# A first transfer and a narrow transfer: w2 ahead of wq, and the tail of w1 on 16 partitions

## The chip, the cores and the metric

The kernel runs on one core of one Trainium2 chip. The metric is the device time of one execution in microseconds (us). The six runs of the kernel before lie between 214.81 and 215.13 us (0.15%). A transfer into on-chip memory goes to partitions (the 128 rows of a tile). In the traces it is carried in packets, and most transfers end on 16 DMA engines (the last one of w4 leaves 16 landing records, from 209.43 to 211.38 us).

## The reference, cut to what matters

A decode step for 4 sequences: attention over the last 2048 positions of a cached K and V, plus a small MLP branch. The outputs are summed.

```python
xn = layernorm(x)                                   # x: [4, 1, 576]
out = x + A(xn, k_cache, v_cache, wq, wo) + B(xn, w1, w2, w3, w4)
# A: q = xn @ wq (576 x 4096); 32 query heads, 16 KV heads of 128; softmax; @ wo
# B: h = gelu(layernorm(x) @ w1)                    # w1: 576 x 576
#    pads and slices of h along S = 1, then @ w2    # w2: 576 x 576
#    x1 = x + ...;  x1 + gelu(layernorm(x1) @ w3) @ w4
```

With S = 1 the shifted slices of h are zero, so the product with w2 uses a zero operand. The kernel still loads w1 and w2 and does the matmuls. About 88.5 MB are read, and nearly all of it is K and V.

## The kernel before: the parts that matter

Each engine has a list of operations, sorted by `key`. One queue (SP) issues almost all transfers, in the order of their keys. Weights with 576 rows are split into 512 rows, four per partition, and a tail of 64 rows. The tails of w1 and w2 share one tile: w1's rows on even partitions, w2's on odd ones.

```python
w1main = w4_t[:, 0:4 * D].rearrange("p (r n) -> p r n", r=4)      # D = 576
rag12 = w4_t[:, 8 * D:9 * D]
...
def rag_pair(tile, even, odd):
    return [(tile[p:128:2, 0:w.shape[1]], w[512:576, :]) for p, w in enumerate((even, odd))]
...
ev_wq = [add_dma([(kt_t[:], A_wq[0:512, :].rearrange("(p r) n -> p (r n)", r=4))], "wq", (), -60),
         add_dma(rag_pair(ragq3, B_w3, A_wq), "wqr", ["ragq3_zero"], -59)]
ev_r12 = add_dma(rag_pair(rag12, B_w1, B_w2), "r12", (), -58.5)
ev_w2 = add_dma([(w2main, B_w2[0:512, :].rearrange("(p r) n -> p r n", r=4))], "w2", (), -58)
ev_w3 = add_dma([...], "w3", (), -57)
ev_w1 = add_dma([...], "w1", (), -56)
... # then K (16 transfers of 2 MB), V (16), wo (2), w4 (5, of falling size)

def pe_h(h):                      # h = xn2 @ w1, half h of the columns
    def f(e):
        for r in range(4):
            e.matmul(HTps[h], lhsT=xn2T[:, r, :], rhs=w1main[:, r, HALF * h:HALF * (h + 1)], start=(r == 0), stop=False)
        return e.matmul(HTps[h], lhsT=xn2T[:, 4, :], rhs=rag12[:, HALF * h:HALF * (h + 1)], start=False, stop=True)
    return f
```

## Time and profile before

| | before |
|---|---|
| time, median of 6 runs | 214.96 us |
| span of the profiled run | 213.6 us |
| share of 16 DMA engines' span, queue 1 | 97.8% |
| bytes read | 88.49 MB |
| landings of the last w4 transfer on its 16 engines: first, mean, last | 209.43, 210.40, 211.38 us |

The page of the kernel before, in 40 slices of 5.3 us: the digits are busy tenths (9 is 90% or more); the GB/s row is what the DMA engines moved; then come the DMA queues with packets, MB and share.

```profile
DMA  7999989999999999999999999999999999999993
GB/s 270 418 380 507 442 359 436 417 428 423 426 430 426 423 430 436 422 430 426 433 426 430 430 422 427 430 420 433 430 423 426 430 433 426 426 429 439 422 406 130
...
q1 hardware_dynamic: 6520, 88.50, 97.8%
q8 instruction: 8, 0.13, 0.2%
q14 instruction: 2, 0.02, 0.0%
```

The DMA row is unbroken. What ends last is therefore a DMA engine, and the chain of waits says so (start, length, what):

```profile
178.09 32.22 DMA w<-in_B_w_dram
210.31 0.04 issue
210.36 1.40 PE ps L431 x18
211.75 0.43 DVE out_sb L548
```

The timeline of before shows the first issues, q's matmuls, the second pass with w3 (it waited 2.0 us for w3), the first K transposes, and at the end the weight load that waited for the last packet of w4:

```profile
0.81 0.41 SPq L176 DMA_DIRECT2D kt<-in_A_wq_dram  x1
13.42 3.60 PE L293 MATMUL ps<-kt,xnT 128*32 128x512 bf16 x32
28.51 4.70 PE L511 MATMUL ps<-w,x1nT 128*32 128x387 bf16 x69 [2.04 <-DMA w<-in_B_w_dram]
36.36 1.95 PE L333 MATMUL ps<-perm_bf,ring 128*128 128x128 bf16 x32
...
211.42 0.08 PEld L431 LDWEIGHTS ps<-w,h2T_sb 128*4 128x4 bf16 x2 [0.24 <-DMA w<-in_B_w_dram]
```

The averages of the page hide one thing. The trace also records every DMA packet (start, duration, size) and every landing (read here as one per DMA engine and transfer: 16 records for w2 or w3; five for x, four of them at 7.91 to 8.27 us and one at 3.16 us, before its data moved at 6.32). On one engine, each packet starts 3 or 4 ns before the one ahead of it ends, so a packet chain can be followed. In these traces each engine is then a serial worker with fixed periods: 47 ns for a packet of 1152 bytes, 174 ns for 4608, 0.61 us for 16 KB, about 1.22 us for 32 KB. A late engine doesn't catch up: the spread of the landings stays between 1.93 and 1.98 us from the K transfer at 49 us to the end. The 16 landings of the last w4 transfer, in ns after the first of them, were:

```
before: 0 18 28 199 257 367 377 856 1405 1520 1583 1620 1645 1833 1909 1951
```

The kernel ends with the slowest of these 16. The two large groups in that list come from the instruction queue (q8 in the page): each 16 KB packet of it sets one engine back by about 1.55 us.

### The profile page before, as it was taken

How to read it: one execution, taken by the hardware profiler on the slowest of the kernel's cores; microseconds unless marked ns; L12 is line 12 of the kernel's file. 1: busy time of each engine (PE TensorE's matmuls, PEld its weight loads, DVE VectorE, ACT ScalarE, POOL GpSimd, SP SyncE). 2: the span in 40 equal slices, each digit the busy share in tenths (PEclk: the TensorE clock that was granted, in tenths of full speed). 3: DMA queues.
4: the chain of work that ended last, by engine and by line, in shares of the span. 5: the costliest groups of instructions: out<-in, count | busy, mean ns of one | idle time of the engine just before them, and what ended most of it. 6: DMA issues, size and time to landing. Idle time of an engine off the chain costs nothing. (4 is left out here: it accounts for less than half of the span.)

```text
span 213.6 us, 5903 instructions
## 1 busy us (share of the span) xinstructions
PE 142.3 (67%) x2664; PEld 110.4 (52%) x2668; DVE 75.2 (35%) x147; ACT 61.8 (29%) x76; POOL 10.9 (5%) x38
## 2 busy tenths in 40 slices
PE   0058469999999999999996178033444433336995
PEld 0023256877778887888874058033434433334542
DVE  0332701666666666666664840100010001001000
ACT  2001204666555665666666530000000000000000
POOL 8301000000000000000000000000000000000000
PEclk9999959999999999999999555555555555555799
DMA  7999989999999999999999999999999999999993
GB/s 270 418 380 507 442 359 436 417 428 423 426 430 426 423 430 436 422 430 426 433 426 430 430 422 427 430 420 433 430 423 426 430 433 426 426 429 439 422 406 130
DMA packets 6546, 88.65 MB, mean 415 GB/s; under 512 B 764, under 2 KB 1032, under 8 KB 1544
## 3 DMA queue, kind: packets, MB, share of 16 engines
q1 hardware_dynamic: 6520, 88.50, 97.8%
q8 instruction: 8, 0.13, 0.2%
q14 instruction: 2, 0.02, 0.0%
q10 hardware_dynamic: 16, 0.01, 0.0%
HBM read 88.49 MB, written 0.00 MB: 414 GB/s over the span
## 5 line engine op out<-in xcount | busy, mean ns | idle before, releaser
L333 PE MATMUL ps<-perm_bf,ring 128*128 128x128 bf16 x1024 | 62.5, 219 | 1.3 <-PEq L572 0.3
L333 PEld LDWEIGHTS ps<-perm_bf,ring 128*128 128x128 bf16 x1024 | 57.5, 98 | 10.7 <-issue 10.7
L340 DVE COPY kt<-ps 128x1024 bf16<-128x1024 bf16 x80 | 52.3, 687 | 27.2 <-PE ps L333 27.2
L339 ACT ACTIVATE kt<-ps 128x1024 bf16<-128x1024 bf16 x48 | 49.2, 1024 | 30.8 <-PE ps L333 29.5
L414 PE MATMUL ps<-PTpad,ring 128*128 128x8 bf16 x1024 | 29.6, 168 | 41.2 <-PEq L572 37.6
L414 PEld LDWEIGHTS ps<-PTpad,ring 128*128 128x128 bf16 x1024 | 28.7, 104 | 42.3 <-issue 42.2
L549 ACT ACTIVATE out_sb<-ps 4x288 bf16<-4x288 f32 x1 | 0.4, 402 | 87.2 <-PE ps L431 87.2
L347 PE MATMUL ps<-kt,Qs 128*32 128x512 bf16 x272 | 17.8, 382 | 1.4 <-PEq L572 1.4
L403 DVE TENSOR_TENSOR PTpad<-PT,mU_bf 128x512 bf16<-128x512 bf16 x16 | 6.4, 421 | 29.4 <-PE ps L414 29.4
L426 DVE TENSOR_TENSOR OTn<-ps,rinvB 128x32 bf16<-128x32 f32 x4 | 0.8, 191 | 34.5 <-PE ps L414 34.5
L347 PEld LDWEIGHTS ps<-kt,Qs 128*32 128x32 bf16 x272 | 5.7, 95 | 6.8 <-issue 1.5
L274 PE MATMUL ps<-ident_bf,xn_bf 4*128 4x4 bf16 x8 | 0.6, 170 | 12.9 <-DVE ragsrc L268 12.9
L368 POOL COPY Qs<-Qpad 128x128 bf16<-128x128 bf16 x16 | 4.6, 296 | 86.9 <-PE ps L347 73.6
L511 PE MATMUL ps<-w,x1nT 128*32 128x387 bf16 (+7 forms) x90 | 5.9, 404 | 2.3 <-DMA w<-in_B_w_dram 2.0
L274 PEld LDWEIGHTS ps<-ident_bf,xn_bf 4*128 4x128 bf16 x8 | 0.4, 112 | 12.9 <-issue 10.5
L511 PEld LDWEIGHTS ps<-w,x1nT 128*32 128x32 bf16 x90 | 4.5, 124 | 3.6 <-DMA w<-in_B_w_dram 2.3
L431 PE MATMUL ps<-w,ORT 128*4 128x288 bf16 x64 | 5.5, 345 | 0.4 <-DVE ORT L453 0.4
L548 DVE CAST out_sb<-ps 4x288 bf16<-4x288 f32 x1 | 0.4, 446 | 14.5 <-PE ps L431 14.5
L431 PE MATMUL ps<-w,h2T_sb 128*4 128x288 bf16 x72 | 5.0, 286 | 0.7 <-DMA w<-in_B_w_dram 0.7
L385 PE MATMUL ps<-kt,permT_bf 128*128 128x512 bf16 x3 | 1.8, 607 | 4.9 <-DVE kt L384 4.8
L261 ACT ACTIVATE sd<-mv 4x1 f32<-4x1 f32 x3 | 0.6, 202 | 14.8 <-DVE mv L259 14.8
L431 PEld LDWEIGHTS ps<-w,ORT 128*4 128x4 bf16 x64 | 3.3, 102 | 2.9 <-DVE ORT L453 1.0
(99 smaller groups left out, 65.8 us busy)
## 6 DMA issues: line engine op xcount, KB each, us to landing
ring<-in_A_k_cache_dram SPq DMA_DIRECT2D x16, 2048.0 KB, 14.5
ring<-in_A_v_cache_dram SPq DMA_DIRECT2D x16, 2048.0 KB, 17.4
w<-in_B_w_dram SPq DMA_DIRECT2D x1, 4608.0 KB, 24.0
w<-in_A_wo_dram SPq DMA_DIRECT2D x2, 2304.0 KB, 20.9
kt<-in_A_wq_dram SPq DMA_DIRECT2D x1, 4096.0 KB, 12.3
w<-in_B_w_dram SPq DMA_DIRECT2D x1, 2592.0 KB, 28.0
w<-in_B_w_dram SPq DMA_DIRECT2D x3, 576.0 KB, 13.7
w<-in_B_w_dram SPq DMA_DIRECT2D x1, 1296.0 KB, 30.6
```

The source lines that it names most:

```text
L274: e.transpose(XTps[idx][:, r, :], v[:, r, :], ident_bf[0:B, 0:B])
L333: ins = e.transpose(tb[n % 4][:, t, :], slot_t(c)[:, 8 * k + t, :], perm_bf[:])
L339: return "act", lambda e: e.activation(out=ktbuf[:, n % 16], in_=tb[n % 4], func=ACTF.Copy)
L340: return "dve", lambda e: e.tensor_copy(out=ktbuf[:, n % 16], in_=tb[n % 4])
L347: ins = e.matmul(Sps[32 * u:32 * u + 32, q, :].rearrange("p (t i) -> p t i", t=16), lhsT=Qs[:, c % NPOS, 32 * u:32 * u + 32], rhs=ktgrp[:, ...
L368: P(lambda e, c=c, cc=cc: e.tensor_copy(out=Qs[:, c % NPOS, :], in_=Qpad_t[:, 128 * cc:128 * cc + 128]), waits=["qT", "qs_zero"] + ([f"SC{ ...
L385: add("pe", lambda e, q=q: e.matmul(ps[:, 4 + q % 3, :], lhsT=permT_bf[:], rhs=PTx[:, q, :], start=True, stop=True), waits=[f"PTx{q}", "pe ...
L403: return lambda e: e.tensor_tensor(out=PTpad[:, c % 2], in0=PTv[:, :, cc, :].unsqueeze(2).to_broadcast([128, NT, NU, 2]), in1=mU_bf[:].uns ...
L414: ins = e.matmul(o_, lhsT=slot_t(c)[:, t, :], rhs=PTpad[:, c % 2, t].rearrange("p u e -> p (u e)"), start=(t == 0), stop=(t == NT - 1))
L426: add("dve", lambda e, hv=hv: e.tensor_tensor(out=hv(OTn), in0=OTps.rearrange("p (b h) -> p b h", b=B), in1=hv(rinvB), op=ALU.mult), waits ...
L431: return e.matmul(ACC[h], lhsT=lhsT, rhs=rhs, start=start, stop=stop, tile_position=(0, 32 * h), skip_group_check=True)
L511: ins = e.matmul(H2ps[k][32 * g:32 * g + 32, :].rearrange("p (x c) -> p x c", c=9)[:, :, off:off + cnt], lhsT=x_, rhs=w[:, base_:base_ + 1 ...
```

## The change

Its intent is to have small packets first, and to take bytes off the DMA engines that end last. It has two parts. w2's 512 rows are issued first. The 64 last rows of w1 go to 16 partitions (4 rows on each), read with an outermost dimension of 4. The second part needs more matmuls of 16 rows each, more transposes, and a memset of the tile that w2's tail now has alone.

```diff
+        w1rag = w4_t[0:16, 18 * D:22 * D]
...
-        xn2T = sb("xn2T", [128, 5, B], BF16)
+        xn2T = sb("xn2T", [128, 8, B], BF16)
...
+        P(lambda e: e.memset(rag12[:], 0.0), sig="rag12_zero", key=-98)
...
-        ev_r12 = add_dma(rag_pair(rag12, B_w1, B_w2), "r12", (), -58.5)
-        ev_w2 = add_dma([(w2main, ...)], "w2", (), -58)
+        ev_r12 = add_dma([(w1rag, B_w1[512:576, :].rearrange("(b a c) n -> a b (c n)", b=4, a=4)),
+                          (rag12[1:128:2, :], B_w2[512:576, :])], "r12", ["rag12_zero"], -58.5)
+        ev_w2 = add_dma([(w2main, ...)], "w2", (), -61)
...   (the last 64 columns of xn2 are reordered to match; 4 transposes of 16 columns replace 1 of 128)
-                return e.matmul(HTps[h], lhsT=xn2T[:, 4, :], rhs=rag12[...], start=False, stop=True)
+                for c in range(4):
+                    ins = e.matmul(HTps[h], lhsT=xn2T[0:16, 4 + c, :], rhs=w1rag[:, c * D + HALF * h:c * D + HALF * (h + 1)],
+                                   start=False, stop=(c == 3))
```

More of the change, by code (lines that the diff above doesn't have):

```diff
@@ L146, in bass_parallel_sum__sliding_block_cached__mixer_s_mlp__decode_kernel @@
         HTps = [ps[0:B, 2 + k, 0:HALF] for k in range(2)]
-        XTps = [ps[:, k, a:a + 10].bitcast(BF16).rearrange("p (c b) -> p c b", b=B) for k, a in ((3, 300), (7, 0), (7, 12))]
+        XTps = [ps[:, k, a:a + 16].bitcast(BF16).rearrange("p (c b) -> p c b", b=B) for k, a in ((3, 300), (7, 0), (7, 20))]
         S = {}
@@ L218, in bass_parallel_sum__sliding_block_cached__mixer_s_mlp__decode_kernel @@
                  add_dma(rag_pair(ragq3, B_w3, A_wq), "wqr", ["ragq3_zero"], -59)]
-        ev_r12 = add_dma(rag_pair(rag12, B_w1, B_w2), "r12", (), -58.5)
-        ev_w2 = add_dma([(w2main, B_w2[0:512, :].rearrange("(p r) n -> p r n", r=4))], "w2", (), -58)
+        ev_r12 = add_dma([(w1rag, B_w1[512:576, :].rearrange("(b a c) n -> a b (c n)", b=4, a=4)),
+                          (rag12[1:128:2, :], B_w2[512:576, :])], "r12", ["rag12_zero"], -58.5)
+        ev_w2 = add_dma([(w2main, B_w2[0:512, :].rearrange("(p r) n -> p r n", r=4))], "w2", (), -61)
         ev_w3 = add_dma([(w3_t[:], B_w3[0:512, :].rearrange("(p r) n -> p (r n)", r=4))], "w3", (), -57)
@@ L266, in ln_ops @@
                                                  op0=ALU.subtract, op1=ALU.mult), waits=[f"{tag}_rstd"], sig=f"{tag}_n", key=k0 + 0.04)
-            odd = int(idx == 0)
-            add("dve", lambda e: e.tensor_copy(out=ragsrc[:, idx, odd:128:2], in_=dst[:, 512:D]), waits=[f"{tag}_n", "rag_zero"], sig=tag, key=k0 + 0.05)
+            r_out, r_in = ragsrc[:, idx, int(idx == 0):128:2], dst[:, 512:D]
+            if idx == 1:
+                r_out = ragsrc[:, idx, 0:64].rearrange("q (c a b) -> q c a b", c=4, a=4)
+                r_in = r_in.rearrange("q (b a c) -> q c a b", b=4, a=4)
+            add("dve", lambda e: e.tensor_copy(out=r_out, in_=r_in), waits=[f"{tag}_n", "rag_zero"], sig=tag, key=k0 + 0.05)
         def pe_xT(src, idx):
@@ L274, in f @@
                     e.transpose(XTps[idx][:, r, :], v[:, r, :], ident_bf[0:B, 0:B])
-                return e.transpose(XTps[idx][:, 4, :], ragsrc[:, idx, :], ident_bf[0:B, 0:B])
+                if idx != 1:
+                    return e.transpose(XTps[idx][:, 4, :], ragsrc[:, idx, :], ident_bf[0:B, 0:B])
+                for c in range(4):
+                    ins = e.transpose(XTps[idx][0:16, 4 + c, :], ragsrc[:, idx, 16 * c:16 * c + 16], ident_bf[0:B, 0:B])
+                return ins
             return f
@@ L280, in bass_parallel_sum__sliding_block_cached__mixer_s_mlp__decode_kernel @@
         add("pe", pe_xT(xn_bf, 0), waits=["ident_bf", "ln1"], sig="xT", key=-40)
-        add("dve", lambda e: e.tensor_copy(out=xnT[:, :, 0:B], in_=XTps[0]), waits=["xT", "xnT_zero"], sig="xnT", key=-39)
+        add("dve", lambda e: e.tensor_copy(out=xnT[:, :, 0:B], in_=XTps[0][:, 0:5, :]), waits=["xT", "xnT_zero"], sig="xnT", key=-39)
         def pe_q(r):
@@ L313, in bass_parallel_sum__sliding_block_cached__mixer_s_mlp__decode_kernel @@
         add("pe", pe_xT(xn2_bf, 1), waits=["ln2", "ident_bf"], sig="x2T", key=-36)
-        add("dve", lambda e: e.tensor_copy(out=xn2T[:], in_=XTps[1]), waits=["x2T"], sig="xn2T", key=-25)
+        add("dve", lambda e: e.tensor_copy(out=xn2T[:, 0:4, :], in_=XTps[1][:, 0:4, :]), waits=["x2T"], sig=None, key=-25)
+        add("dve", lambda e: e.tensor_copy(out=xn2T[0:16, 4:8, :], in_=XTps[1][0:16, 4:8, :]), waits=["x2T"], sig="xn2T", key=-24.9)
         def pe_zero(e):
@@ L471, in f @@
                     e.matmul(HTps[h], lhsT=xn2T[:, r, :], rhs=w1main[:, r, HALF * h:HALF * (h + 1)], start=(r == 0), stop=False)
-                return e.matmul(HTps[h], lhsT=xn2T[:, 4, :], rhs=rag12[:, HALF * h:HALF * (h + 1)], start=False, stop=True)
+                for c in range(4):
+                    ins = e.matmul(HTps[h], lhsT=xn2T[0:16, 4 + c, :], rhs=w1rag[:, c * D + HALF * h:c * D + HALF * (h + 1)], start=False, stop=(c == 3))
+                return ins
             return f
@@ L490, in bass_parallel_sum__sliding_block_cached__mixer_s_mlp__decode_kernel @@
         add("pe", pe_xT(x1n_bf, 2), waits=["ln3", "xn2T"], sig="x1T", key=-23)
-        add("dve", lambda e: e.tensor_copy(out=x1nT[:, :, 0:B], in_=XTps[2]), waits=["x1T", "x1nT_zero"], sig="x1nT", key=-23)
+        add("dve", lambda e: e.tensor_copy(out=x1nT[:, :, 0:B], in_=XTps[2][:, 0:5, :]), waits=["x1T", "x1nT_zero"], sig="x1nT", key=-23)
         for h in range(2):
```

## The prediction

> **What bounds the kernel.** The 16 DMA engines. The DMA row of the 40 slices is 9 in all but three slices, queue 1 takes 97.8% of 16 engines' span, and the windows view shows a DMA share of 0.96 to 1.01 until 178 us. The packet records show no engine idle between the first packets (1.8 to 2.3 us) and the last landings (209.4 to 211.4 us). The chain of waits ends in 32 us of w4 transfer, 1.4 us of last matmuls, 0.43 us of copy, then the output. The time is start, plus the packets of the slowest DMA engine, plus that tail.
>
> The engines do not end together: the 16 landings of the last w4 transfer spread over 1.95 us. A 16 KB packet of the instruction queue (8 in the trace) sets the one engine that carries it back by about 1.55 us, an 8 KB one by 0.6 to 1.0 us, and this is never made up.
>
> **What the change does, in DMA.** Bytes are equal. Order: w2 (8 packets of 4608 bytes per engine, 174 ns apart, 1.4 us) goes ahead of wq. The tail of w1 was 4 packets of 1152 bytes on each of 16 engines (47 ns apart, 0.19 us); now it is 16 packets of 4608 bytes. [...] No trace has shown this transfer yet; the load of x (4 packets of 1152 bytes) is one that uses 4 engines. So four engines get 4 x 174 = 0.70 us instead of 0.19 (+0.51 us), twelve get 0.19 us less. Following the packets end to start, the four engines of x end about 0.4, 0.9, 1.4 and 1.6 us after the first of the last landings, one less certain; the latest (1.95) is not among them. Estimate: the latest moves from 1.95 to about 2.1 (1.6 + 0.51), +0.1 to +0.2 us; -0.19 if none of the four is late, up to +0.5 if one is among the very latest.
>
> w2 first: the first packet of each engine takes 1.6 to 2.2 us for what later takes 1.22. I take that excess as a start latency any first packet pays: 0, give or take 0.15 us.
>
> **What it does on the engines.** q waits for wq: its matmuls start at 13.4 us, so q, its transposes, hs and ln3 come about 1.4 us later. The second h2 pass waits for w3 anyhow (28.5 us, 2 us idle before it), so this is hidden; w3 itself lands within 0.5 us of before. The tail of w1 takes 8 matmuls instead of 2 (about 0.2 us each at the reduced clock), 3 more transposes, one more copy (0.15 us): K transposes start 1 to 2 us after 36.3. Slot 0 then is free near 43 us instead of 41.2; the fourth K transfer lands at 49 us, so the queue never runs dry. The added memset on POOL (about 0.6 us) ends before SP reaches its wait. Nothing of this is on the critical path.
>
> **Prediction.** 215.0 us, 8 in 10 between 214.6 and 215.5. Faster by over 2%: 0.01; within 2%: 0.98; slower: 0.01.
>
> **What would show it.** Sixteen 4608-byte packets for the tail of w1, on four engines; w1's landings spread wider by 0.7 us (four late); the DMA row unbroken; q's matmuls near 14.8; h2's second pass near 28.5 to 29; the last w4 landing 0.1 to 0.2 us later.
>
> **What would make it wrong.** Instruction packets landing on other engines; a first transfer of small packets starting noticeably faster or slower; writes to 16 partitions being slower than 174 ns a packet.

The number of engines of the new tail was the author's assumption, with the load of x as the nearest thing in the trace of before (four packets, and the landings told above). 214.85 us (the median of the three runs known then), plus about 0.15 (1.6 + 0.51 against 1.95), plus 0 for the start, is 215.0.

## The result, and the profile after

| | time, median (runs) | before in the same rounds | ratio, 95% interval |
|---|---|---|---|
| after, first measured | 214.77 us (6) | 214.96 us (6) | 0.9990 (0.9977 to 1.0003) |
| after, measured again (e10) | 214.73 us (5) | 215.04 us (9) | 0.9985 (0.9972 to 0.9999) |

All ratios here are the mean time of one kernel's runs over that of the other's of the same rounds, so they are not quite the ratio of the medians quoted. The time fell by 0.2 to 0.3 us, one part in a thousand. That is close to the noise: the first interval includes no change, the second just excludes it. The time lies inside the predicted range. The predicted shift, however, was upward (214.85 was the median of the three runs known then, 215.0 predicted), and the measured one is downward: the range was wide enough to hold both. Two steps of the forecast were wrong, and the experiments were made to find them.

The page of after, the same rows:

```profile
DMA  7999999999999999999999999999999999999993
GB/s 295 406 398 477 435 382 439 418 428 421 436 424 424 430 436 421 422 436 427 427 427 439 421 438 419 427 421 427 433 430 427 424 430 427 436 431 419 434 408 117
...
q1 hardware_dynamic: 6460, 88.50, 97.7%
q8 instruction: 8, 0.13, 0.2%
q14 instruction: 2, 0.02, 0.0%
```

The bytes are the same, in 60 packets fewer. The first slice moves 295 GB/s instead of 270. The timeline of after:

```profile
0.81 0.41 SPq L177 DMA_DIRECT2D w<-in_B_w_dram  x1
2.24 0.58 POOL L197 MEMSET w<- 128x576 bf16 x1
14.46 3.17 PE L303 MATMUL ps<-kt,xnT 128*32 128x512 bf16 x32
28.51 4.88 PE L524 MATMUL ps<-w,x1nT 128*32 128x387 bf16 x69 [2.92 <-DMA w<-in_B_w_dram]
37.33 1.95 PE L344 MATMUL ps<-perm_bf,ring 128*128 128x128 bf16 x32
...
211.25 0.08 PEld L442 LDWEIGHTS ps<-w,h2T_sb 128*4 128x4 bf16 x2 [0.22 <-DMA w<-in_B_w_dram]
```

q starts 1.0 us later. The second w3 pass starts at the same 28.51 us, because it waited for w3 in both. The K transposes start 1.0 us later. At the end nothing of that is left: the last weight load comes 0.17 us earlier, when the last packet of w4 does. So the engines' work moved by a microsecond and the time followed the DMA engines alone. The chain of waits of after, as printed, runs along PE from 193 us on, but it ends in the same pieces, and the load at 211.25 us is released by the DMA.

```profile
210.19 1.39 PE ps L442 x18
211.58 0.44 DVE out_sb L561
```

From the packet and landing records of the two traces (us):

| | before | after |
|---|---|---|
| mean landing of w3 (the same bytes were queued ahead of it) | 28.22 | 27.95 |
| last w4 transfer: first, mean, last landing | 209.43, 210.40, 211.38 | 208.98, 210.09, 211.21 |
| packets of 1152 bytes in w1's tail | 64 on 16 engines | none |
| packets of 4608 bytes in w1's tail | none | 16 on 4 engines |

The mean engine gains 0.27 us by 28 us and keeps it (0.31 us at the end). The bytes of the mean engine are unchanged, so this gain lies in the start. The last engine gains only 0.17 us. In the after trace that engine belongs to three chains that started their first K packet within 5 ns of each other, so which of them it was can't be said from that trace alone.

### The profile page after: what moved, and what is told of

The parts are those of the page before. It is cut to its first block, busy times and chain, and to the rows that moved or that the text cites. A ratio compares the mean times of both kernels' runs of the same rounds, so it can differ in the third digit from the quotient of the medians.

```text
span 213.4 us, 5927 instructions
## 1 busy us (share of the span) xinstructions
PE 142.9 (67%) x2677; PEld 110.9 (52%) x2677; DVE 75.3 (35%) x148; ACT 61.4 (29%) x76; POOL 11.4 (5%) x39
## 5 line engine op out<-in xcount | busy, mean ns | idle before, releaser
L344 PE MATMUL ps<-perm_bf,ring 128*128 128x128 bf16 x1024 | 61.8, 219 | 0.9 <-PEq L585 0.3
L350 ACT ACTIVATE kt<-ps 128x1024 bf16<-128x1024 bf16 x48 | 48.6, 1023 | 30.2 <-PE ps L344 29.4
L524 PE MATMUL ps<-w,x1nT 128*32 128x387 bf16 (+7 forms) x90 | 6.8, 437 | 3.2 <-DMA w<-in_B_w_dram 2.9
L524 PEld LDWEIGHTS ps<-w,x1nT 128*32 128x32 bf16 x90 | 5.0, 133 | 4.7 <-DMA w<-in_B_w_dram 3.2
L442 PE MATMUL ps<-w,ORT 128*4 128x288 bf16 x64 | 6.2, 373 | 0.4 <-DVE ORT L464 0.4
L396 PE MATMUL ps<-kt,permT_bf 128*128 128x512 bf16 x4 | 2.4, 608 | 4.3 <-DVE kt L395 4.1
```

Source lines behind the costliest of these rows:

```text
L344: ins = e.transpose(tb[n % 4][:, t, :], slot_t(c)[:, 8 * k + t, :], perm_bf[:])
L350: return "act", lambda e: e.activation(out=ktbuf[:, n % 16], in_=tb[n % 4], func=ACTF.Copy)
L396: add("pe", lambda e, q=q: e.matmul(ps[:, 4 + q % 3, :], lhsT=permT_bf[:], rhs=PTx[:, q, :], start=True, stop=True), waits=[f"PTx{q}", "pe ...
L442: return e.matmul(ACC[h], lhsT=lhsT, rhs=rhs, start=start, stop=stop, tile_position=(0, 32 * h), skip_group_check=True)
L524: ins = e.matmul(H2ps[k][32 * g:32 * g + 32, :].rearrange("p (x c) -> p x c", c=9)[:, :, off:off + cnt], lhsT=x_, rhs=w[:, base_:base_ + 1 ...
```

## The experiments

Each was timed in 5 rounds, beside before. The first four ran on one chip, the last seven on another.

| run | what it is | median (runs) | before, same rounds | ratio (95% interval) | mean landing of w3 | last w4: mean, last |
|---|---|---|---|---|---|---|
| e1 | w2 first only | 214.88 (6) | 215.07 (11) | 0.9992 (0.9980 to 1.0004) | 28.01 | 210.19, 211.23 |
| e2 | four-engine tail only | 214.88 (5) | 215.07 (11) | 0.9990 (0.9977 to 1.0003) | 28.24 | 210.42, 211.58 |
| e3 | after, tail with an outermost dimension of 16 | 215.53 (5) | 215.07 (11) | 1.0022 (1.0009 to 1.0035) | 28.71 | 210.91, 212.15 |
| e4 | before, small piece of wq first | 214.70 (5) | 215.07 (11) | 0.9986 (0.9973 to 0.9999) | 28.11 | 210.29, 211.18 |
| e5 | after, 72 KB more on the four | 215.02 (5) | 215.00 (9) | 1.0003 (0.9989 to 1.0016) | 28.11 | 210.28, 211.44 |
| e6 | before, 72 KB more to adjacent partitions | 215.68 (5) | 215.00 (9) | 1.0029 (1.0015 to 1.0042) | 28.82 | 211.00, 212.17 |
| e7 | before, 72 KB more to spread partitions | 215.47 (5) | 215.00 (9) | 1.0023 (1.0009 to 1.0037) | 28.56 | 210.74, 211.91 |
| e8 | before, large piece of wq first | 215.07 (5) | 215.00 (9) | 1.0002 (0.9988 to 1.0015) | 28.36 | 210.39, 211.48 |
| e9 | e4 and the four-engine tail | 214.70 (5) | 215.04 (9) | 0.9986 (0.9973 to 1.0000) | 28.07 | 210.24, 211.22 |
| e10 | after again | 214.73 (5) | 215.04 (9) | 0.9985 (0.9972 to 0.9999) | 27.90 | 210.08, 211.16 |
| e11 | e9, smaller first piece | 214.97 (5) | 215.04 (9) | 0.9998 (0.9984 to 1.0011) | 28.43 | 210.56, 211.49 |

All outputs are right. w3's landing is comparable where the bytes ahead of it are equal (e5 to e7 have 72 KB more), and in e8 and e11 an instruction packet came before w3's last landing and adds about 0.1 us to the mean (1.55 us on one of 16 engines).

### The two parts alone: e1 and e2

e1 is before with `"w2", (), -58` set to `-61`.

> The kernel before with one part of the change: w2 is the first transfer, the tail of w1 is left as it was. Theory A (the two parts are separate gains): w2 first shortens the start of the DMA engines. In the traces of before and after, the mean engine has lost 2.86 us and 2.62 us by its first K packet against an undisturbed stream; so all 16 landings of the last w4 transfer should come about 0.24 us earlier on average (mean 210.40 us before, so about 210.16) and the time should fall by 0.15 to 0.3 us. Theory B (everything comes from w2 first, the four-engine tail costs something): the same here or a little more, 0.2 to 0.4 us below before, and below after. Theory C (the 0.24 us is a chance of two single traces): same mean landing as before within 0.05 us and no gain in time.

e2 is after with `"w2", (), -61` set back to `-58`.

> The kernel before with the other part alone: the tail of w1 by one transfer on four engines, w2 in its old place. Theory A: 12 engines carry 0.19 us less, four carry 0.51 us more, the mean landing of the last w4 transfer stays at 210.40 us, the last landing comes 0.19 us earlier (211.38 to 211.19), because no 16 KB instruction packet falls on the four: time lower by 0.1 to 0.2 us. Theory B: one of the four carries a 16 KB instruction packet (in the trace of before one of them seemed to), so the last landing comes at 211.4 to 211.7 and the time is 0 to 0.4 us above before.

e1 did what theory A says: the mean landing of w3 moved from 28.22 to 28.01 us, that of the last w4 from 210.40 to 210.19, and the median lies 0.19 us lower. The earlier start stays to the end.

e2's median is also 0.19 us lower, as theory A says, and its mean landing (210.42) is unmoved, as it must be. Its last landing (211.58) looks like theory B, but the packet records say otherwise. The profiled run was the slowest of the five (215.20 us, the others 214.74 to 215.02). Followed packet by packet, the engine that ends last is one of the twelve: its first packet took 2.64 us and ended at 4.62, while before the latest of the first packets ended at 4.20. (This chain and one of the four run 6 ns apart; the usual overlap of 3 or 4 ns tells which is which.) The latest of the four is done 0.34 us ahead of it. The four are the engines that loaded x, and they carry the two 8 KB instruction packets and none of 16 KB. So the trace supports the mechanism of theory A, while its last landing missed theory A's 211.19. The sum of the two medians' gains is 0.38 us, and the whole change gave 0.19 and 0.31 us. With intervals of 0.13% (0.28 us) on each ratio, that is consistent with two separate gains, but it does not show that they add fully. Each of the two ratios alone is also consistent with no change.

### Is it the size of the first packets? e4 and e8

e4 leaves the order alone and cuts wq into two transfers:

```diff
-[(kt_t[:], A_wq[0:512, :].rearrange("(p r) n -> p (r n)", r=4))]
+[(kt_t[:, x:y], A_wq[0:512, :].rearrange("(p r) n -> p (r n)", r=4)[:, x:y])
+ for x, y in ((0, 2304), (2304, 16384))]
```

e8 is the same with `((0, 14080), (14080, 16384))`, so the large piece comes first.

> The kernel before, with the order of transfers unchanged, but wq in two transfers: the first 4608 bytes of each partition, then the other 28160. So the first packets of each engine have the size of those of w2, and are of wq. Theory A, in the form that the size of the first packets makes the start shorter (first 32 KB packets took 1.94 us where later ones take 1.22; eight first 4608-byte packets lost 0.45 us in all): mean loss by the first K packet near 2.6 us, mean landing near 210.2 us, time 0.15 to 0.3 us below before, as with w2 first. Rival D (it is w2's place in memory or the order that matters, not the size): loss 2.85 us as before, no gain.

> Control of e4: wq in two transfers as there, but the large piece first (28160 bytes of each partition, then 4608). If the size of the first packets shortens the start, this gains nothing: within 0.1 us of before, mean loss by the first K packet 2.8 to 2.9 us, and 0.2 to 0.3 us above e4. If the gain of e4 came from two transfers in place of one, this one is as fast as e4.

e4 is 0.37 us faster by medians (0.15 to 0.3 expected), e8 0.07 us slower (within 0.1 expected). Both have two transfers for wq, and only the order of the pieces differs. So the gain is tied to the small first packets, not to having two transfers. The packet records show it where it arises. Before, the first packet of each engine (32 KB) took 1.94 us in the mean, where later ones take 1.22, so 0.72 us are lost. In after, the first five packets of 4608 bytes took 433, 303, 209, 209 and 184 ns in the mean against 178, so 0.45 us are lost. Two traces alone would be a thin basis, since this loss differs from run to run: 0.49 to 0.72 us where the first packets are large, 0.20 to 0.59 where they have 4608 bytes. Surer is the whole loss at the start, which includes the time before the first packet: the mean time at which the first packet of each engine, or its eight small ones, are done, less what they usually take. It is 2.69 to 2.81 us in the five runs with a large first packet (before, e2, e6, e7, e8), and 2.32 to 2.61 in the seven that begin with 4608 bytes.

Within these seven, w2 first lost 2.32 to 2.51 us, and the small piece of wq (e4, e9) 2.61 and 2.58. So by the traces the small piece gives about half of what w2 first gives, and rival D is not excluded for the other half. The traces also give e4 less than its median does (w3's mean landing 0.11 us earlier, the last landing 0.20). Part of its advantage in time may be chance.

### Do the four engines have room? e5

e5 is after with the four-engine transfer a second time, to an unused place:

```diff
                           (rag12[1:128:2, :], B_w2[512:576, :]),
+                          (w4_t[32:48, 22 * D:26 * D], B_w1[512:576, :].rearrange("(b a c) n -> a b (c n)", b=4, a=4))], "r12", ["rag12_zero"], -58.5)
```

> The kernel after [...]: the same four-engine transfer of w1's tail a second time, to an unused place (partitions 32 to 47). Four engines carry 0.70 us more, twelve carry nothing more. Theory A (no 16 KB instruction packet falls on the four; in the trace of after their slowest ends 0.4 us before the last): time 0.2 to 0.5 us above after, and in the packet records the four chains, now set apart, carry only the two 8 KB instruction packets. Theory B (one of the four is the last engine): time 0.7 us above after, and a 16 KB instruction packet on one of the four chains.

0.70 us more on each of four engines cost 0.2 to 0.4 us: against before, e5 is at 1.0003, and after at 0.9990 and 0.9985. In its trace the last landing is 211.44 us, 0.23 us after that of after. So the four had about 0.45 us of room (0.70 less 0.23). This is theory A.

The run also settles which engines carry the instruction packets. The four chains are now set apart: they start their first K packet at 30.02 us or later, all undisturbed others by 29.33. (One more engine is at 30.19, delayed by the first 16 KB packet at 28.0 us. It is not one of the four, which would have been near 31.5 with it.) Of the seven later 16 KB packets, six fell on chains that had started by 29.33 and carried none before, and the last, at 208.9 us, followed an engine that had just finished, while none of the four can finish before about 210 (an undisturbed chain ends 180 us after its first K packet). The two 8 KB packets fell on chains of the late group. So the two small instruction packets fall on the four engines, and all the large ones on the twelve others, as in e2's trace.

### Why not 16 engines for the narrow tile? e3, e6 and e7

e3 keeps the 16 partitions and the matmuls of after, but reads the tail with an outermost dimension of 16, expected to run on 16 engines (no landing count of e3, e6 or e7):

```diff
-(w1rag, B_w1[512:576, :].rearrange("(b a c) n -> a b (c n)", b=4, a=4))
+(w1rag, B_w1[512:576, :].rearrange("(p c) n -> p (c n)", c=4))
```

> The kernel after with the same 16 partitions and the same 8 matmuls, but the tail of w1 read with an outermost dimension of 16 (partition p holds rows 4p to 4p+3), so that it should run on 16 engines, one 4608-byte packet each (0.174 us against 0.19). Theory A: the 12 late engines get their 0.17 us back, so the last landing and the time are 0.1 to 0.2 us above after. Theory B: the four engines lose 0.53 us each, so the time is equal to after or up to 0.3 us below it. The matmuls are those of after, so a difference to after is of the DMA engines alone.

Neither theory holds here: e3 is 0.46 us slower than before, about 0.7 us slower than after. Its engines' means are late (210.91 us), not only its last one. The windows view shows where. Columns are the stretch, its length, busy time of the engines, granted clock, DMA share and GB/s. First after, then e3:

```profile
13.40:16.00 2.60, 1.93 (x24) 0.98 (x28) 0.58 (x2) 0.00 (x0) 0.00 (x0) 1.00 0.98 410
16.00:18.00 2.00, 2.00 (x28) 0.67 (x20) 0.00 (x0) 0.00 (x0) 0.00 (x0) 1.00 1.29 541
```

```profile
13.40:16.00 2.60, 1.95 (x24) 0.97 (x28) 0.54 (x2) 0.00 (x0) 0.00 (x0) 1.00 0.97 397
16.00:18.00 2.00, 2.00 (x24) 0.69 (x20) 0.00 (x0) 0.00 (x0) 0.00 (x0) 1.00 1.28 410
```

(Packets count in the stretch in which they start, hence shares over 1.) From 16 to 18 us the DMA engines of e3 were just as busy as those of after and moved a quarter less. In the packet records, the tail's packets took up to 160 ns longer than 178, and w3's first packets up to 0.83 us longer than 1.36. In all, 10.4 us of engine time went to slow packets (here and below: over 20 ns longer than usual) after 13.4 us, 0.65 us per engine, against 0.04 in after and none in before.

e6 and e7 ask whether it matters how close together the partitions lie. They add the same 72 KB to before, unused, with the outermost dimension of e3:

```diff
-ev_r12 = add_dma(rag_pair(rag12, B_w1, B_w2), "r12", (), -58.5)
+ev_r12 = add_dma(rag_pair(rag12, B_w1, B_w2) + [(w4_t[32:48, 22 * D:26 * D],
+                  B_w1[512:576, :].rearrange("(p c) n -> p (c n)", c=4))], "r12", (), -58.5)
```

e7 has `w4_t[0:128:8, ...]` in its place. So e6 writes 16 adjacent partitions, and e7 16 that lie 8 apart.

> Why was the 16-engine form of the tail slow (e3: 0.46 us above before)? In its trace, packets between 16.3 and 17.6 us took up to 0.8 us longer. The kernel before with an extra 16-engine load of 72 KB to 16 adjacent partitions (32 to 47), unused. Theory E (16 engines that write to the same few adjacent partitions hold each other up): 0.17 us of packets per engine plus 0.4 to 0.6 us of slow packets, so 0.5 to 0.8 us above before. Rival F (e3 lost its time by something else, the new order or the matmuls): 0.1 to 0.25 us above before and no slow packets beside this transfer.

> The partner of e6: the same extra 72 KB from the same source on 16 engines, but to partitions 0, 8, 16 and so on to 120. Theory E: only the packets' own time, 0.1 to 0.25 us above before, no slow packets. Rival F: the same time as e6.

e6 cost 0.68 us, and its slow packets make 0.33 us per engine (5.2 us in all), beside 0.17 for its own packet. e7 cost 0.47 us, with 0.08 us per engine of slow packets (1.3 us in all). With every excess counted, however small, it is 0.38 and 0.15 us. So slow packets come with this kind of transfer in the old order too, and without the new matmuls, which rules out rival F for them; and they cost two and a half to four times less where the partitions are spread. That is the order theory E wants. But e7's time missed its band (0.1 to 0.25 us): own packet and slow packets make 0.26 us, and 0.2 us of its 0.47 are not explained, nor 0.2 of e6's 0.68. What the runs show is an order (slow packets per engine after 13.4 us): 0.65 and 0.33 us with 16 adjacent partitions and an outermost dimension of 16 (e3 and e6), 0.08 with partitions 8 apart (e7), none in e2, which has the four-engine tail alone. The 0.04 us of after, and 0.09 of its repeat e10, don't belong in this order: none of it is on the tail, and e1, which has no narrow tail, has 0.04 too. The trace doesn't name the engines, so that they hold each other up, as theory E has it, isn't shown: why the packets were slow stays open. That e3 lost twice as much to them as e6 is open as well.

### Can both be beaten? e9, e10 and e11

e9 joins e4's split to the four-engine tail. e10 is after, repeated for the comparison. e11 is e9 with `((0, 576), (576, 16384))`, so 1152 bytes per partition first.

> A candidate that should beat both kernels: wq in two transfers, the 4608-byte piece of each partition first (as e4, w2 in its old place), and the tail of w1 on four engines (as after). If the shorter start and the balance are both real and independent, it has the start of e4 (about 0.25 to 0.35 us off) and the 0.19 us off the twelve engines: 0.3 to 0.5 us below before, so about 0.1 to 0.3 us below after, and the last landing near 211.0 us. If one of the two covers the other, it is equal to after or to e4 within 0.1 us.

> The kernel after again, unchanged, for a comparison on the same chip in the same rounds: 0.1 to 0.3 us below before.

> As e9, with a first piece of 1152 bytes per partition. If smaller first packets shorten the start further, 0.1 us below e9; if the eight small packets are used up before the engines run at rate (eight times 47 ns is less than the 0.45 us that the start still loses), the next packets of 31 KB pay it: equal to e9 or 0.1 to 0.2 us above it.

e9 (214.70 us) and e10 (214.73) are equal, so the hoped-for 0.1 to 0.3 us below after did not come. The split and w2 first are two ways to a gain in time of the same size. e9 is not faster than e4 either, which lacks the four-engine tail (0.9986 both): added to e4, the tail gained nothing that the times can show. e11 has lost it again: it is 0.07 us below before, and its last w4 landings (210.56 us in the mean, 211.49 the last) are no earlier than those of before (210.40 and 211.38). Its expectation says why it could be so (eight packets of 47 ns are 0.38 us, less than the 0.45 us that the start loses), but no packet times of its start are on record, so the reason isn't shown. In these runs the gain came with eight first packets of 4608 bytes per engine (1.4 us), and not with eight of 1152 bytes. No run beats after by more than the noise. After, e4 and e9 are the best.

## Why the prediction was right and wrong

- **What bounds the kernel** was right. q, h and the K transposes moved by 1 us and the time did not follow. The memset took 0.58 us (about 0.6 predicted), q's matmuls began at 14.46 us (near 14.8), the eight matmuls of the tail took 0.65 us for each four with 0.99 of the clock granted from 34.1 to 36 us, so about 0.16 us each (about 0.2 at a reduced clock predicted), the second w3 pass at 28.51 us (28.5 to 29), the K transposes 1.0 us later (1 to 2).
- **How the tail runs** was right: sixteen packets of 4608 bytes on four engines. Four was assumed, and the trace of after shows it: with an outermost 4 the 16 packets form four chains of four, 174 ns apart, that start at 16.15, 16.16, 16.25 and 16.29 us, and the semaphore of the two tail transfers shows 21 landing records in place of 32, one of them at 4.19 us, before any of the tail's data moved. The four chains are those that also loaded x: followed from end to start (3 or 4 ns), the packets of x at 6.19, 6.28, 7.42 and 7.55 us lead to these four, as in e2's trace. One sign was less clean: w1's landings spread over 0.48 us before, and over 0.85 in after without the engine that an instruction packet delayed, with no group of four apart.
- **"w2 first: ... I take that excess as a start latency any first packet pays: 0, give or take 0.15 us"** was the step that failed most. The excess differed with the size of the first packets: 0.72 us with 32 KB, 0.45 with eight of 4608 bytes in these two traces, and the whole loss at the start separates the two kinds in all twelve (2.69 to 2.81 us against 2.32 to 2.61). Measured alone, w2 first moved the mean landing by 0.21 us (e1), and e4 against e8 ties it, at least in part, to the small packets. Why a large first packet loses more is not settled. A fixed latency alone would cost both the same.
- **"The latest moves from 1.95 to about 2.1"** was the second step that failed. It rested on one of the four engines carrying a 16 KB instruction packet. I had said "one less certain": at that packet two chains ended within 1 ns of each other, and I took the wrong one. e5, which sets the four apart, shows no 16 KB packet on them. The alternative in the text ("-0.19 if none of the four is late") is the case that the traces of e2 and e5 show; e2's median is 0.19 us lower, within its noise.
- The predicted +0.15 us thus became -0.2 to -0.3: about -0.2 by the start and up to -0.19 by the balance. The first part is shown by the traces of twelve runs. The second is argued from three traces and not shown by the times: e2's interval includes no change, and e9 is not faster than e4. By the prediction's own figures it would have been smaller, since the engine of x that ended at 1.4 us would end at 1.91 with 0.51 more, against 1.95. In the traces of after and e2, though, the latest of the four was done 0.40 and 0.34 us before the last engine. The whole gives slightly less than the sum. In the first after trace the slowest engine carried a large instruction packet, so by e5 it is the one of the three tied chains that belongs to the twelve. That chain had its first packet at 2.62 us, 0.6 us after the mean, and lost about 0.4 us more to slow packets before K. The rest is within the noise of the medians and is left open.

## What to carry to other kernels

When the DMA row has no gaps, ask when the slowest of the 16 engines ends: the landings of the last transfer give it in one line, and here the outermost dimension of a small transfer moved bytes from twelve engines to four (0.19 us less on each of the twelve, 0.51 more on each of the four; what that gained lies within the noise). Try a first transfer of small packets that lasts about as long as the start: 1.4 us of 4608-byte packets came with a gain here, 0.4 us of 1152-byte packets did not. When two engines' chains tie in a trace, don't rest a forecast on which is which; an extra load that sets the engines in question apart costs one run and answers it.
